# Mish dense layer, 2048 x 512 x 1792: x tiles 2-3 by DMA transpose, eight f tiles first, w1 mostly on the other DMA ring

## Chip, cores, metric

The kernel runs on one core of a Trainium2 chip. The metric is device microseconds (us) of one execution. A profiled execution has a span, which is about 1.4 us shorter than its time. Times within a profile are counted from the start of its span.

## The reference

```python
# x (1, 2048, 512), w1 (512, 1792), b1 (1792), w2 (1792, 512), all bfloat16
def reference(x, w1, b1, w2):
    h = jnp.einsum("bsd,df->bsf", x, w1) + b1
    sp = jnp.log1p(jnp.exp(-jnp.abs(h))) + jnp.where(h > 0, h, jnp.zeros_like(h))
    act = h * jnp.tanh(sp)                 # Mish
    return jnp.einsum("bsf,fd->bsd", act, w2)
```

## The kernel before

The kernel does x in four blocks of 512 rows. For each block it computes `mm1` (w1 against transposed x, 14 f tiles of 4 k steps, 512 columns each), Mish on ScalarE (ACT), then `mm2` (16 matmul chains in all, 14 f steps each). TensorE (PE) needs x transposed. Blocks 1 to 3 come transposed by DMA. Block 0, which everything starts with, is loaded as it is, transposed by TensorE tile by tile (128 rows) and copied out of PSUM by VectorE (DVE) and ACT in turn.

Loads go out on two queues, one issued from SyncE (SP) and one from ACT; I call them the SP ring and the ACT ring. Every load has its own semaphore. A load returns a token, and an engine that needs the data waits on that token:

```python
def wait(self, *tokens):                       # in class Stream
    for tok in tokens:
        ...                                    # cut: None is skipped, known values too
        self.eng.wait_ge(sem, v)

t_xa = load(sp, x_nat[:, 0, :], x0v[0], "s_xa")
t_w1k = [load(act, w1_sb[:, 0:2, 0:F0 * P], w1v[:, 0:2, 0:F0 * P], "s_w1k0")] * 2
t_xb = load(sp, x_nat[:, 1, :], x0v[1], "s_xb")
t_w1k += [load(act, w1_sb[:, 2:4, 0:F0 * P], ..., "s_w1k2")] * 2
t_xc = load(sp, x_nat[:, 2:4, :], x0v[2], "s_xc")
...                                            # cut: b1 on ACT; w1 f 4-7 and f 8-13 on SP
t_w2 = load(sp, w2_sb[:, :, :], w2v, "s_w2")
t_xT = [None]
for s in range(1, NSB):
    t_xT.append(load(sp, xT[:, :, s * SBW:(s + 1) * SBW], x2[s * SBW:(s + 1) * SBW, :], "s_xT%d" % s, True))
```

`t_xT` is a list with one token for each block. In the steady loop `mm1(t)` waits for `t_xT[s]`, the one of its own block. The head of block 0 is written out:

```python
first_mm1([0], by_k(0, 1))                     # four f tiles, x tile 0
part_T([1], t_xb)                              # transpose x tile 1
first_mm1([1], by_k(0, 1))
first_mm1([0, 1], by_k(2))
part_T([2, 3], t_xc)                           # transpose x tiles 2-3
first_mm1([0, 1], by_k(3))
first_mm1([2, 3], by_k(0, 1) + [(f, k) for f in range(F0) for k in (2, 3)])
...                                            # cut: b1 transposed, mish of f 0-3
for t in range(F0, FT):
    mm1(t)                                     # f 4-13, 512 columns each
```

Of the kernel before, what the change touches and what calls it, by code (L numbers as in the profile page):

```python
# [4 lines left out]

P = 128
N_WARM = 16
N_FILL = 3


class Stream:
# [20 lines left out]
def bass_standalone__dense_activation_mish__prompt_kernel(  # L32
# [8 lines left out]
    ACT = mybir.ActivationFunctionType  # L41
    ALU = mybir.AluOpType
    BF, F32 = dt.bfloat16, dt.float32

    _, S, D = x.shape
    F = w1.shape[1]
    KT, FT, SBW = D // P, F // P, 512
    NSB, JT = S // SBW, SBW // P
    assert (S, D, F) == (2048, 512, 1792)
    x2, out2 = x[0], out[0]  # L50
    w1v = w1.rearrange("(k p) f -> p k f", p=P)
    w2v = w2.rearrange("(j p) d -> p j d", p=P)
    F0 = 4

    with ExitStack() as es:
        def sb(name, shape, t):
            return es.enter_context(nc.sbuf_tensor(name, shape, t))

        x_nat = sb("x_nat", [P, JT, D], BF)
        xT = sb("xT", [P, KT, S], BF)  # L60
        w1_sb = sb("w1_sb", [P, KT, F], BF)
        w2_sb = sb("w2_sb", [P, FT, D], BF)
        b1_nat = sb("b1_nat", [FT, P], BF)
        b1_sb = sb("b1_sb", [P, FT], F32)
        ones = sb("ones", [P, P], BF)
        ident = sb("ident", [P, P], BF)
        a_sb = sb("a_sb", [P, NSB * FT, SBW], BF)
        o_sb = sb("o_sb", [P, NSB * JT, D], BF)
        ps = es.enter_context(nc.psum_tensor("ps", [P, 8, 512], F32))

        def sem(name):
            return es.enter_context(nc.semaphore(name))

        sp = Stream(nc.sync, None)
        pe = Stream(nc.tensor, sem("c_pe"))
        dve = Stream(nc.vector, sem("c_dve"))
        act = Stream(nc.scalar, sem("c_act"))
        pool = Stream(nc.gpsimd, sem("c_pool"))

        def load(q, dst, src, name, transpose=False):  # L80
            s = sem(name)
            (q.eng.dma_start_transpose if transpose else q.eng.dma_start)(dst, src).then_inc(s, 16)
            return (s, 16)

        n_pre = len(nc.cur_bb.bb.instructions)



        x0v = [x2[0:P, :], x2[P:2 * P, :], x2[2 * P:SBW, :].rearrange("(p j) d -> p j d", j=2)]
        t_xa = load(sp, x_nat[:, 0, :], x0v[0], "s_xa")  # L90
        t_w1k = [load(act, w1_sb[:, 0:2, 0:F0 * P], w1v[:, 0:2, 0:F0 * P], "s_w1k0")] * 2
        t_xb = load(sp, x_nat[:, 1, :], x0v[1], "s_xb")
        t_w1k += [load(act, w1_sb[:, 2:4, 0:F0 * P], w1v[:, 2:4, 0:F0 * P], "s_w1k2")] * 2
        t_xc = load(sp, x_nat[:, 2:4, :], x0v[2], "s_xc")
        t_b1 = load(act, b1_nat[:, :], b1.rearrange("(j p) -> j p", p=P), "s_b1")
        t_w1 = {}
        for a, b in ((4, 8), (8, FT)):
            t = load(sp, w1_sb[:, :, a * P:b * P], w1v[:, :, a * P:b * P], "s_w1_%d" % a)
            for f in range(a, b):
                t_w1[f] = t  # L100
        t_w2 = load(sp, w2_sb[:, :, :], w2v, "s_w2")
        t_xT = [None]
        for s in range(1, NSB):
            t_xT.append(load(sp, xT[:, :, s * SBW:(s + 1) * SBW], x2[s * SBW:(s + 1) * SBW, :], "s_xT%d" % s, True))

# [5 lines left out]
        act.eng.preload_act_table(ACT.Mish)  # L111


        warm = sb("warm", [P, P], BF)
        pe.wait(dve.mark(nc.vector.memset(warm[:, :], 1.0)))  # L115

        def dummies(n):
            for _ in range(n):
                nc.tensor.matmul(ps[:, 7, 0:P], warm[:, :], warm[:, :], start=True, stop=True)  # L119

        t_cp, t_mm1 = {}, {}
        n_cp = 0

        def part_T(js, tok):

            nonlocal n_cp
            lo, hi = js[0] * P, (js[-1] + 1) * P
            pe.wait(tok)
            for k in range(KT):
                pe.wait(t_cp.get((js[0] - 1, k)))  # L130
                psk = ps[:, k, 0:(hi - lo) // 2].bitcast(BF)
                for n, j in enumerate(js):
                    tr = nc.tensor.transpose(psk[:, n * P:(n + 1) * P], x_nat[:, j, k * P:(k + 1) * P], ident[:, :])  # L133
                t = pe.mark(tr)
                dst = xT[:, k, lo:hi]
                if k % 2 == 0:
                    dve.wait(t)
                    t = dve.mark(nc.vector.tensor_copy(dst, psk))  # L138
                else:
                    act.wait(t)  # L140
                    t = act.mark(act.eng.activation(dst, psk, ACT.Copy))  # L141
                for j in js:
                    t_cp[j, k] = t

        def first_mm1(js, fks):


            cs = slice(js[0] * P, (js[-1] + 1) * P)
            for f, k in fks:
                pe.wait(t_w1k[k], *[t_cp[j, k] for j in js])  # L150
                mm = nc.tensor.matmul(ps[:, 4 + f, cs], w1_sb[:, k, f * P:(f + 1) * P], xT[:, k, cs],  # L151
                                      start=(js[0] == 0 and k == 0), stop=(js[-1] == JT - 1 and k == KT - 1))
                if js[-1] == JT - 1 and k == KT - 1:
                    t_mm1[f] = pe.mark(mm)

        def by_k(*ks):
            return [(f, k) for k in ks for f in range(F0)]

        dummies(N_WARM)
        pe.wait(t_id)  # L160
        part_T([0], t_xa)
        dummies(N_FILL)


        t_mish, t_bank = {}, {}

        def bank1(t):
            return t - F0 if F0 <= t < 2 * F0 else 4 + t % 4

        def mish(t, t_mm):  # L170
            act.wait(t_b1c, t_mm)
            f = t % FT
            t_mish[t] = act.mark(act.eng.activation(a_sb[:, t, :], ps[:, bank1(t), :], ACT.Mish, bias=b1_sb[:, f:f + 1]))  # L173
            t_bank[bank1(t)] = t_mish[t]

        def mm1(t):
            s, f = divmod(t, FT)
            pe.wait(t_bank.get(bank1(t)), t_w1.get(f), t_xT[s])
            for k in range(KT):
                mm = nc.tensor.matmul(ps[:, bank1(t), :], w1_sb[:, k, f * P:(f + 1) * P],  # L180
                                      xT[:, k, s * SBW:(s + 1) * SBW], start=(k == 0), stop=(k == KT - 1))
            mish(t, pe.mark(mm))

        def store(q, i, lo, hi, tok):
            q.wait(tok)
            rows = o0v[:, i % 2, :] if i in (2, 3) else out2[i * P:(i + 1) * P, :]
            q.eng.dma_start(rows[:, lo:hi], o_sb[:, i, lo:hi]).then_inc(s_out, 16)

        s_out = sem("s_out")
        o0v = out2[2 * P:SBW, :].rearrange("(p j) d -> p j d", j=2)  # L190
        n_out = 0

        LC = 384
# [1 line left out]
        def mm2(i):  # L195
            nonlocal n_out
            s, j = divmod(i, JT)
            pe.wait(t_w2)
            last = i == NSB * JT - 1
            parts = [(0, LC, i % 4), (LC, D, (i + 1) % 4)] if last else [(0, D, i % 4)]  # L200
            for lo, hi, bank in parts:
                pe.wait(t_bank.get(bank))
                for f in range(FT):
                    t = s * FT + f
                    pe.wait(t_mish[t])
                    mm = nc.tensor.matmul(ps[:, bank, 0:hi - lo], a_sb[:, t, j * P:(j + 1) * P], w2_sb[:, f, lo:hi],  # L206
                                          start=(f == 0), stop=(f == FT - 1))
                t_mm = pe.mark(mm)
                dve.wait(t_mm)
                t_bank[bank] = dve.mark(nc.vector.tensor_copy(o_sb[:, i, lo:hi], ps[:, bank, 0:hi - lo]))  # L210
                store(sp, i, lo, hi, t_bank[bank])
                n_out += 1


        first_mm1([0], by_k(0, 1))
        part_T([1], t_xb)
        first_mm1([1], by_k(0, 1))
        first_mm1([0, 1], by_k(2))
        part_T([2, 3], t_xc)
        first_mm1([0, 1], by_k(3))  # L220
        first_mm1([2, 3], by_k(0, 1) + [(f, k) for f in range(F0) for k in (2, 3)])
        for k in range(KT):
            t_bank[k] = t_cp[JT - 1, k]
        pe.wait(t_b1, t_bank[3])
        psb1 = ps[:, 3, 0:FT // 2].bitcast(BF)
        dve.wait(pe.mark(nc.tensor.transpose(psb1, b1_nat[:, :], ident[0:FT, 0:FT])))  # L226
        t_bank[3] = t_b1c = dve.mark(nc.vector.tensor_copy(b1_sb[:, :], psb1))  # L227
        for f in range(F0):
            mish(f, t_mm1[f])
        for t in range(F0, FT):  # L230
            mm1(t)
        for s in range(NSB):
            for j in range(JT):
# [41 lines left out]
```

## Time and profile before

| What | Before |
|---|---|
| Time, median of 6 (range) | 105.92 us (105.08 to 106.06) |
| Span of the profiled execution | 103.9 us |
| TensorE busy | 101.1 us, 97% |
| First `mm2` matmul in the chain of waits | 17.41 us |

The page of the kernel before gives busy time by engine, then the span in 40 slices with the busy share in tenths. PEclk is the granted TensorE clock in tenths.

```profile
PE 101.1 (97%) x513; PEld 50.0 (48%) x522; DVE 13.0 (12%) x25; ACT 40.4 (39%) x63; POOL 0.6 (1%) x6
...
PE   8999999999999999999999999999999999999992
...
PEclk9999999999999999999999999999999999999999
```

TensorE is busy everywhere; only the head can give something. The head is read from the timeline (start, duration, engine, line, operation, count) of the kernel before:

```profile
2.28 0.58 PE L133 MATMUL ps<-ident,x_nat 128*128 128x128 bf16 x4
...
3.15 1.03 PE L151 MATMUL ps<-xT,w_sb 128*128 128x128 bf16 x8
...
5.77 0.61 PE L133 MATMUL ps<-ident,x_nat 128*128 128x128 bf16 x8
...
6.22 2.35 PE L151 MATMUL ps<-xT,w_sb 128*128 128x256 bf16 x20
```

Transposes are L133 and the head's own matmuls L151. The next lines are from its chain of waits (start, duration, what):

```profile
8.83 8.58 PE ps L180 x39
17.41 2.16 PE ps L206 x10
```

Line L206 is `mm2`. The first block's `mm1` is worth 56 matmuls of about 0.214 us, which is 12.0 us; TensorE starts on the first x tile at 2.28. That leaves 17.41 - 2.28 - 12.0 = 3.1 us of overhead in the head.

### The profile page before, as it was taken

Reading aid. Unit: us, or ns where it says so; the run is one execution under the profiler, and the core shown is the slowest. Engines: PE = TensorE matmul, PEld = TensorE weight load, DVE = VectorE, ACT = ScalarE, POOL = GpSimd, SP = SyncE. Lnnn points to the kernel's source line nnn. Section 1 sums busy time; section 2 is a strip of 40 time slices with the busy share of each in tenths; the row PEclk is TensorE's granted clock in tenths of the full one; section 3 lists DMA queues with packets and bytes.
Section 4 is the critical chain, followed back from the end, with each engine's and each line's share of the span. In section 5 each row is a group of like instructions: output and inputs, shape, how many; then the busy total and the mean of one; then the engine's idle time right before and its main releaser. Section 6 shows DMA issues by size and latency. Waiting matters only on the chain.

```text
span 103.9 us, 1168 instructions
## 1 busy us (share of the span) xinstructions
PE 101.1 (97%) x513; PEld 50.0 (48%) x522; DVE 13.0 (12%) x25; ACT 40.4 (39%) x63; POOL 0.6 (1%) x6
## 2 busy tenths in 40 slices
PE   8999999999999999999999999999999999999992
PEld 7895444444444444444444444444444444444462
DVE  0310000112220000022220000022112000011223
ACT  2525997000027777200007777500005777700000
POOL 2000000000000000000000000000000000000000
PEclk9999999999999999999999999999999999999999
DMA  5999996951101000010111000001111000001111
GB/s 169 294 349 376 349 187 149 260 146 50 50 7 43 0 6 0 0 50 14 37 50 50 0 3 6 0 0 50 50 50 50 0 0 0 0 6 50 50 50 51
DMA packets 12561, 7.94 MB, mean 76 GB/s; under 512 B 6796, under 2 KB 12428, under 8 KB 12556
## 3 DMA queue, kind: packets, MB, share of 16 engines
q1 hardware_dynamic: 11984, 7.34, 26.5%
q10 hardware_dynamic: 572, 0.53, 1.5%
q8 instruction: 4, 0.07, 0.3%
q14 instruction: 1, 0.01, 0.0%
HBM read 4.20 MB, written 2.10 MB: 61 GB/s over the span
## 4 chain that ended last, share of the span: by engine, by line
PE 97%; issue 1%; DVE 0%
PE ps L206 46%; PE ps L180 43%; PE ps L151 4%; PE ps L119 2%; PE ps L133 1%; DVE o_sb L210 0%; DVE warm L115 0%; PE ps L226 0%
## 5 line engine op out<-in xcount | busy, mean ns | idle before, releaser
L173 ACT ACTIVATE a_sb<-ps,b_sb 128x512 bf16<-128x512 f32 x56 | 37.5, 691 | 46.3 <-PE ps L180 44.2
L206 PE MATMUL ps<-w_sb,a_sb 128*128 128x512 bf16 (+2 forms) x234 | 48.8, 366 | 0.2
L180 PE MATMUL ps<-xT,w_sb 128*128 128x512 bf16 x203 | 45.1, 379 | 0.4 <-issue 0.2
L206 PEld LDWEIGHTS ps<-w_sb,a_sb 128*128 128x128 bf16 x238 | 22.8, 98 | 25.9
L180 PEld LDWEIGHTS ps<-xT,w_sb 128*128 128x128 bf16 x208 | 20.3, 98 | 24.3
L210 DVE CAST o_sb<-ps 128x512 bf16<-128x512 f32 (+2 forms) x17 | 11.2, 660 | 82.3 <-PE ps L206 82.3
L151 PE MATMUL ps<-xT,w_sb 128*128 128x256 bf16 (+1 forms) x40 | 4.7, 282 | 0.0
L151 PEld LDWEIGHTS ps<-xT,w_sb 128*128 128x128 bf16 x40 | 3.7, 113 | 0.7 <-DVE xT L138 0.3
L119 PE MATMUL ps<-warm 128*128 128x128 bf16 x19 | 2.4, 310 | 0.4 <-DVE warm L115 0.4
L141 ACT ACTIVATE xT<-ps 128x128 bf16<-128x128 bf16 (+1 forms) x6 | 1.6, 311 | 2.1 <-PE ps L133 2.1
L119 PEld LDWEIGHTS ps<-warm 128*128 128x128 bf16 x19 | 2.0, 143 | 0.4 <-DVE warm L115 0.4
L138 DVE COPY xT<-ps 128x128 bf16<-128x128 bf16 (+1 forms) x6 | 1.4, 247 | 4.9 <-PE ps L133 4.9
L111 ACT ACT_TABLE_LOAD x1 | 1.3, 1283 | 1.8 <-issue 1.8
L133 PE MATMUL ps<-ident,x_nat 128*128 128x128 bf16 x16 | 1.8, 263 | 0.0
L133 PEld LDWEIGHTS ps<-ident,x_nat 128*128 128x128 bf16 x16 | 1.3, 118 | 0.3 <-issue 0.2
L227 DVE CAST b_sb<-ps 128x14 f32<-128x14 bf16 x1 | 0.2, 173 | 2.1 <-PE ps L226 2.1
L109 POOL TENSOR_SCALAR_AFFINE_SELECT ident<-ones 128x128 bf16<-128x128 bf16 x1 | 0.3, 295 | 0.1
L107 POOL MEMSET ones<- 128x128 bf16 x1 | 0.2, 205 | 0.0
L226 PEld LDWEIGHTS ps<-ident,b_nat 14*128 14x128 bf16 x1 | 0.1, 90 | 0.2 <-issue 0.2
L115 DVE MEMSET warm<- 128x128 bf16 x1 | 0.2, 165 | 0.2 <-issue 0.2
L226 PE MATMUL ps<-ident,b_nat 14*128 14x14 bf16 x1 | 0.2, 177 | 0.0
L260 POOL MEMSET const-bfloat16-1.0<- 128x1 bf16 x1 | 0.1, 103 | 0.0
(3 smaller groups left out, 0.3 us busy)
## 6 DMA issues: line engine op xcount, KB each, us to landing
out_dram<-o_sb SPq DMA_DIRECT2D x15, 128.0 KB, 1.7
w_sb<-in_w_dram SPq DMA_DIRECT2D x1, 1792.0 KB, 12.7
w_sb<-in_w_dram SPq DMA_DIRECT2D x1, 768.0 KB, 8.2
w_sb<-in_w_dram ACTq DMA_DIRECT2D x2, 256.0 KB, 3.6
w_sb<-in_w_dram SPq DMA_DIRECT2D x1, 512.0 KB, 6.5
x_nat<-in_x_dram SPq DMA_DIRECT2D x2, 128.0 KB, 2.6
x_nat<-in_x_dram SPq DMA_DIRECT2D x1, 256.0 KB, 3.9
out_dram<-o_sb SPq DMA_DIRECT2D x1, 96.0 KB, 1.6
```

What stands on the lines that cost most here:

```text
L109: t_id = pool.mark(pool.eng.affine_select(ident[:, :], ones[:, :], pattern=[[1, P]], compare_op=ALU.is_equal, fill=0.0, base=0, channel_mu ...
L111: act.eng.preload_act_table(ACT.Mish)
L119: nc.tensor.matmul(ps[:, 7, 0:P], warm[:, :], warm[:, :], start=True, stop=True)
L133: tr = nc.tensor.transpose(psk[:, n * P:(n + 1) * P], x_nat[:, j, k * P:(k + 1) * P], ident[:, :])
L138: t = dve.mark(nc.vector.tensor_copy(dst, psk))
L141: t = act.mark(act.eng.activation(dst, psk, ACT.Copy))
L151: mm = nc.tensor.matmul(ps[:, 4 + f, cs], w1_sb[:, k, f * P:(f + 1) * P], xT[:, k, cs], start=(js[0] == 0 and k == 0), stop=(js[-1] == JT ...
L173: t_mish[t] = act.mark(act.eng.activation(a_sb[:, t, :], ps[:, bank1(t), :], ACT.Mish, bias=b1_sb[:, f:f + 1]))
L180: mm = nc.tensor.matmul(ps[:, bank1(t), :], w1_sb[:, k, f * P:(f + 1) * P], xT[:, k, s * SBW:(s + 1) * SBW], start=(k == 0), stop=(k == KT ...
L206: mm = nc.tensor.matmul(ps[:, bank, 0:hi - lo], a_sb[:, t, j * P:(j + 1) * P], w2_sb[:, f, lo:hi], start=(f == 0), stop=(f == FT - 1))
L210: t_bank[bank] = dve.mark(nc.vector.tensor_copy(o_sb[:, i, lo:hi], ps[:, bank, 0:hi - lo]))
L226: dve.wait(pe.mark(nc.tensor.transpose(psb1, b1_nat[:, :], ident[0:FT, 0:FT])))
```

## The change

The intent is to spend less TensorE time on transposes and waits in the head. TensorE transposes only x tiles 0 and 1. Tiles 2-3 come by a small DMA transpose (256 rows). Meanwhile tiles 0-1 are taken against eight f tiles instead of four, k by k, in all eight PSUM banks. The middle part of w1 (f 4-7) moves to the ACT ring, so that the small transpose has less ahead of it on the SP ring. SP holds that transpose back until w1's k 2-3 part has landed. The core of the diff:

```diff
-        t_w1k = [load(act, w1_sb[:, 0:2, 0:F0 * P], w1v[:, 0:2, 0:F0 * P], "s_w1k0")] * 2
+        t_w1k = [load(act, w1_sb[:, k, 0:F0 * P], w1v[:, k, 0:F0 * P], "s_w1k%d" % k) for k in range(2)]
...
+        for k in (0, 2):
+            t_w1m += [load(act, w1_sb[:, k:k + 2, F0 * P:2 * F0 * P], w1v[:, k:k + 2, F0 * P:2 * F0 * P], "s_w1m%d" % k)] * 2
+        sp.wait(t_w1k[2])
+        t_xT = [load(sp, xT[:, :, 2 * P:SBW], x2[2 * P:SBW, :], "s_xT0", True)]
...     # w1 f 8-13, w2 and the transposes of blocks 1-3 follow on the SP ring, appended to t_xT as before
-                pe.wait(t_w1k[k], *[t_cp[j, k] for j in js])
+                pe.wait((t_w1k if f < F0 else t_w1m)[k])
+                if js[0] == 0 and k == 0:
+                    pe.wait(t_bank.get(bank1(f)))
+                pe.wait(*([t_cp[j, k] for j in js] if js[0] < 2 else t_xT))
...
-        first_mm1([0], by_k(0, 1))
-        part_T([1], t_xb)
-        ...
+        first_mm1([0], by_k(0, 0))
+        part_T(1, t_xb)
+        first_mm1([0], by_k(0, 1))
+        first_mm1([1], by_k(0, 0, 1))
+        first_mm1([0, 1], by_k(0, 2))
+        ...     # b1
+        first_mm1([0, 1], by_k(0, 3))
+        ...
+        first_mm1([0, 1], by_k(F0, *range(KT)))
+        first_mm1([2, 3], [(f, k) for f in range(2 * F0) for k in range(KT)])
+        for t in range(2 * F0, FT):
             mm1(t)
```

Cut: `N_FILL` 3 to 2, the copies all on DVE, b1 loaded on the SP ring, plain rows for the output.

## The prediction

> **What bounds the kernel now.** TensorE: busy 101.1 of 103.9 us on the page, 97% of the chain of waits. In steady state 512-column matmuls start about 0.214 us apart with hardly a gap (busy by windows: 59.7 of 60 us), so only the head can give. In the chain mm2 starts at 17.41 us. The first block's mm1 is 56 such matmuls, 12.0 us; x arrives at 2.28. Overhead: 17.41 - 2.28 - 12.0 = 3.1 us. The timeline divides it: transposes 0.58 + 0.43 + 0.45, fillers 0.32, the 16 128-column matmuls about 1.0 over their ideal share (with a wait of 0.26 for a copy), the bias transpose and waits about it 0.27.
>
> The early matmuls are slow by clock: 128-column starts lie 107 ns apart up to about 5.3 us, then 256-column ones take 109 ns. That agrees with the Trainium skill, "TensorE: Matmul & The Clock Gate", Part 1 (half rate until the array has been busy for some microseconds); the page's granted-clock row doesn't show it.
>
> **Removed.** Eight transposes (0.45 us), one filler (0.11), the ACT copies (which waited for the table load and cost PE the 0.26), most of the wait about the bias (0.2). **Added.** 256-column matmuls in place of 512 for eight f tiles: 2 x 109 against 214 ns, about 0.1 us in all. DVE makes all eight copies at 225 ns, behind PE's work.
>
> **Moved.** x tiles 2-3 come by a 256 KB DMA transpose, issued once w1's k 2-3 part has landed (estimate: 4.0 us). The before trace holds three 512 KB transposes: queue time 2.2 and 3.0 us for the two not held up, landing 4.4 and 5.5 us after the start of issue. The first sat in the queue 11.9 us, until the w2 load ahead of it on that ring had drained. Now little is ahead of it on its ring, which is why w1 goes to the other. At half the size I estimate 3 to 4 us from issue: landing at 7.0 to 8.2 us.
>
> PE's timeline from those spacings: first transposes 2.28, first mm1 2.95, tile 1's transposes 3.4, 128-column work till 5.1, 256-column work on tiles 0-1 (24 matmuls) till 7.9. The transposed data is needed at about 7.9 us, nearly when I expect it: a stall of 0 to 0.6 us, 0.2 in the middle. Then 32 x 109 ns and 24 x 214 ns: mm2 starts at 16.6 without a stall, 16.8 with; before 17.4. ACT (691 ns per Mish) falls behind in the k-major stage but frees its banks just in time (f 12's at about 14.7, wanted 14.9). w1's rest (about 10 us, wanted 11.4) and w2 (about 15, wanted 16.6) should be in time.
>
> **Predicted.** The gain is all on the critical path, but only 0.8 us less the stall: 105.1 us, range 104.3 to 106.2. Faster by over 2%: 0.02; within 2%: 0.94; slower by over 2%: 0.04.
>
> **Right or wrong by the profile.** First mm2 at 16.5 to 17.0 in the chain; a wait for the xT DMA of under 0.6 us ahead of the tiles 2-3 matmuls; the small transpose landing 3 to 4 us after issue; no ACT copies; steady state unchanged.
>
> **What would make it wrong.** The transpose held up by the other ring's w1 traffic too, or landing later than 8.5 us: each us late is a us lost, and past 8.8 us the gain is gone. w2 pushed behind 16.6 us. Or the clock rising earlier or later than 5.3 us.

## The result

| What | Before | After |
|---|---|---|
| Time, median of 6 (range) | 105.92 us (105.08 to 106.06) | 122.94 us (122.14 to 124.72) |
| Ratio | | 1.159 (95% interval 1.152 to 1.166) |
| Span of the profiled execution | 103.9 us | 123.1 us (a slow run, 124.48 us) |
| First `mm2` matmul in the chain of waits | 17.41 us | 36.61 us |

A ratio is the mean time of one kernel's fast runs over that of the other's in the same rounds, so it is not quite the ratio of the medians. The outputs of all kernels here are correct.

The page of the changed kernel. Its profiled run is one of the two slow ones (of the six runs, the two more than 1.5% above the fastest); none of its fast runs was traced:

```profile
PE 103.7 (84%) x520; PEld 52.7 (43%) x529; DVE 12.9 (10%) x28; ACT 39.5 (32%) x57; POOL 0.6 (1%) x6
...
PE   8890000089999999999999999999999999999994
...
PEclk9999655555999999999999999999999999999999
```

There is one hole of five slices, and from its second slice on, for six slices, the granted clock is about half. Everything after that is as before. The waits of the changed kernel (who waited for whom: us in total, times, longest):

```profile
PE ps L145 <- DMA xT<-in_x_dram: 16.2, 1, 16.2
```

Its timeline on TensorE:

```profile
2.46 0.59 PE L133 MATMUL ps<-ident,x_nat 128*128 128x128 bf16 x4 [0.18 <-DMA x_nat<-in_x_dram]
...
5.78 1.00 PE L145 MATMUL ps<-xT,w_sb 128*128 128x256 bf16 x4 [0.36 <-DMA w_sb<-in_w_dram]
...
6.67 2.35 PE L145 MATMUL ps<-xT,w_sb 128*128 128x256 bf16 x20
25.21 6.22 PE L145 MATMUL ps<-xT,w_sb 128*128 128x256 bf16 x32 [16.20 <-DMA xT<-in_x_dram]
31.48 5.13 PE L174 MATMUL ps<-xT,w_sb 128*128 128x512 bf16 x23
36.45 3.83 PE L198 MATMUL ps<-w_sb,a_sb 128*128 128x512 bf16 x17
```

The loss is a single wait, ahead of the matmuls on tiles 2-3, and the slow stage after it: 32 matmuls from 25.21 to 31.48, so 196 ns each, where 256 columns take 109 ns at full clock. 16.2 us of stall and 32 x (0.196 - 0.109) = 2.8 us of slow clock make 19.0 of the 19.2 us by which the two spans differ. These are the sizes in a slow run; e2 and e3 below were traced in fast runs and show the same wait and the same slow stage.

Which transfer did it wait for? The page says only "xT". The chain of waits of the changed kernel shows the queue of transposes behind it:

```profile
5.75 1.32 SPq L82
...
8.28 9.94 SPq L82
18.22 0.04 issue
18.27 2.53 SPq L82
20.80 0.04 issue
20.84 4.24 DMA xT<-in_x_dram
25.08 0.14 issue
25.21 6.22 PE ps L145 x32
```

The entry at 5.75 is the small transpose of tiles 2-3; by the trace's landing records it was complete at 9.09, when TensorE had just got there. The wait ended with the entry at 20.84: the transpose of block 3, the last of four. That points to one expression in the diff: `pe.wait(*(... else t_xT))` unpacks the whole list, and when these matmuls are put down the list holds four tokens. So tiles 2-3 of block 0 wait for blocks 1, 2 and 3 as well. The waits of the built program say the same: that matmul waits on `s_xT0`, `s_xT1`, `s_xT2` and `s_xT3`.

### The profile page after: what moved, and what is told of

Its sections match the earlier page's. It is cut to its first block, busy times and chain, and to the rows that moved or that the text cites. A ratio compares the mean times of both kernels' runs of the same rounds, so it can differ in the third digit from the quotient of the medians.

```text
span 123.1 us, 1184 instructions
## 1 busy us (share of the span) xinstructions
PE 103.7 (84%) x520; PEld 52.7 (43%) x529; DVE 12.9 (10%) x28; ACT 39.5 (32%) x57; POOL 0.6 (1%) x6
## 4 chain that ended last, share of the span: by engine, by line
PE 78%; SPq 12%; DMA 7%; issue 1%; ACTq 1%; DVE 0%
PE ps L198 39%; PE ps L174 33%; SPq L82 12%; PE ps L145 5%; DMA w_sb<-in_w_dram 4%; DMA xT<-in_x_dram 3%; ACTq L82 1%; DVE o_sb L202 0%
## 5 line engine op out<-in xcount | busy, mean ns | idle before, releaser
L167 ACT ACTIVATE a_sb<-ps,b_sb 128x512 bf16<-128x512 f32 x56 | 38.2, 687 | 67.8 <-PE ps L174 44.5
L198 PE MATMUL ps<-w_sb,a_sb 128*128 128x512 bf16 (+2 forms) x233 | 48.8, 366 | 0.3
L174 PE MATMUL ps<-xT,w_sb 128*128 128x512 bf16 x188 | 41.7, 379 | 0.2
L198 PEld LDWEIGHTS ps<-w_sb,a_sb 128*128 128x128 bf16 x238 | 22.8, 98 | 25.9
L174 PEld LDWEIGHTS ps<-xT,w_sb 128*128 128x128 bf16 x192 | 18.8, 98 | 22.4
L145 PE MATMUL ps<-xT,w_sb 128*128 128x256 bf16 (+1 forms) x72 | 11.5, 338 | 16.6 <-DMA xT<-in_x_dram 16.2
L145 PEld LDWEIGHTS ps<-xT,w_sb 128*128 128x128 bf16 x72 | 8.4, 128 | 19.2 <-issue 16.4
L134 DVE COPY xT<-ps 128x128 bf16<-128x128 bf16 x8 | 1.2, 217 | 2.8 <-PE ps L133 2.8
L133 PE MATMUL ps<-ident,x_nat 128*128 128x128 bf16 x8 | 1.2, 307 | 0.2 <-DMA x_nat<-in_x_dram 0.2
L133 PEld LDWEIGHTS ps<-ident,x_nat 128*128 128x128 bf16 x8 | 0.8, 137 | 0.4 <-issue 0.4
```

What stands on the lines that cost most here:

```text
L133: dve.wait(pe.mark(nc.tensor.transpose(psk, x_nat[:, j, k * P:(k + 1) * P], ident[:, :])))
L134: t_cp[j, k] = dve.mark(nc.vector.tensor_copy(xT[:, k, j * P:(j + 1) * P], psk))
L145: mm = nc.tensor.matmul(ps[:, bank1(f), cs], w1_sb[:, k, f * P:(f + 1) * P], xT[:, k, cs], start=(js[0] == 0 and k == 0), stop=(js[-1] == ...
L167: t_mish[t] = act.mark(act.eng.activation(a_sb[:, t, :], ps[:, bank1(t), :], ACT.Mish, bias=b1_sb[:, f:f + 1]))
L174: mm = nc.tensor.matmul(ps[:, bank1(t), :], w1_sb[:, k, f * P:(f + 1) * P], xT[:, k, s * SBW:(s + 1) * SBW], start=(k == 0), stop=(k == KT ...
L198: mm = nc.tensor.matmul(ps[:, bank, 0:hi - lo], a_sb[:, t, j * P:(j + 1) * P], w2_sb[:, f, lo:hi], start=(f == 0), stop=(f == FT - 1))
```

## The experiments

The first theory, the "list theory": the loss is the wait for all four transposes, plus the slow clock that the idle time brings. Its rival, the "transpose theory": the small DMA transpose, or the new order of the rings, is itself what is late. The first four kernels tell these apart. The own-wait kernel (e1) came out 0.8% slower than before, not faster, so a second group asks where the predicted 0.8 us went.

| Kernel | Median (us) | Ratio to before, 95% interval |
|---|---|---|
| after | 122.94 | 1.159 (1.152 to 1.166) |
| e1_own_only | 106.47 | 1.008 (1.004 to 1.013) |
| e2_own_and_next | 118.35 | 1.122 (1.115 to 1.128) |
| e3_before_waits_all | 122.33 | 1.157 (1.150 to 1.164) |
| e4_keep_busy | 121.47 | 1.151 (1.145 to 1.157) |
| g1_no_hold | 109.11 | 1.024 (1.017 to 1.031) |
| g2_short_hold | 105.10 | 0.995 (0.990 to 0.999) |
| g3_w2_other_ring | 112.37 | 1.061 (1.055 to 1.068) |
| h1_w2_halves | 105.09 | 0.995 (0.993 to 0.998) |
| h2_w1m_own_ring | 106.60 | 1.006 (1.001 to 1.011) |

The medians are of all runs.

### e1_own_only: wait for the small transpose alone

```diff
-                pe.wait(*([t_cp[j, k] for j in js] if js[0] < 2 else t_xT))
+                pe.wait(*([t_cp[j, k] for j in js] if js[0] < 2 else t_xT[:1]))
```

> The changed kernel, but TensorE waits ahead of the tiles 2-3 matmuls for their own transposed load alone, not for all four transposes. List theory (the stall comes of waiting for the last of four transposes, which lands at 25.1 us in the changed kernel's trace): the wait shrinks from 16.2 us to under 0.5 us (the small transpose landed at 9.05, TensorE was ready at 8.9), the clock stays up, and the time falls to 105.5 to 107.5 us; it need not reach the predicted 105.1, since in that trace w1's last part lands at 13.3 us and would be wanted at 12.6. Transpose theory (the small DMA transpose is itself what came late, or the ring order starves it): the wait stays above 5 us and the time above 112 us.

106.47 us. One token in place of four takes back 16.5 of the 17.0 us. The small transpose lands at 8.47 in this trace, the long wait is gone and the granted clock is 1.0. What is left is a new wait, at the start of `mm2`, on the timeline of this kernel:

```profile
6.03 6.16 PE L145 MATMUL ps<-xT,w_sb 128*128 128x256 bf16 x52
12.21 5.34 PE L174 MATMUL ps<-xT,w_sb 128*128 128x512 bf16 x24
18.74 5.57 PE L198 MATMUL ps<-w_sb,a_sb 128*128 128x512 bf16 x25 [1.20 <-DMA w_sb<-in_w_dram]
```

TensorE waits 1.2 us for w2. The list theory stands; that the change would then win does not.

### e2_own_and_next: wait for two of the four

```diff
-                pe.wait(*([t_cp[j, k] for j in js] if js[0] < 2 else t_xT))
+                pe.wait(*([t_cp[j, k] for j in js] if js[0] < 2 else t_xT[:2]))
```

> The changed kernel, with TensorE waiting for the first two of the four transposes. List theory: the stall ends when the second one lands, at about 20.9 us in the changed kernel's trace (8.28 + 12.6), 4.2 us before the fourth, and the clock is still halved by the long idle time: 118 to 119.5 us. Transpose theory: no change from the 122.9 us.

118.35 us, as the list theory said. The wait in this kernel's timeline:

```profile
19.34 6.37 PE L145 MATMUL ps<-xT,w_sb 128*128 128x256 bf16 x32 [11.18 <-DMA xT<-in_x_dram]
```

It ends at 19.34; the second transpose landed at 19.21 in this trace (I had expected 20.9, from the changed kernel's). The stall follows the last token waited for.

### e3_before_waits_all: the kernel before with the long wait added

```diff
+        pe.wait(*t_xT)
         first_mm1([2, 3], by_k(0, 1) + [(f, k) for f in range(F0) for k in (2, 3)])
```

> The kernel before, untouched but for one wait: TensorE waits for its three transposes (blocks 1 to 3) ahead of the matmuls on tiles 2-3. List theory: the last lands at 22.4 us in the trace of before, TensorE gets there at about 6.9, so 15.5 us of stall and about 3 us of halved clock after it: 122.5 to 125.5 us. If the DMA transpose of tiles 2-3, the k-major order or the moved w1 loads made the loss, this kernel, which has none of them, loses little more than what a late wait costs: under 112 us.

122.33 us, a little under the 122.5 expected. The kernel before, with none of the change in it, becomes as slow as the changed one by this one wait. Its timeline:

```profile
22.29 3.57 PE L151 MATMUL ps<-xT,w_sb 128*128 128x256 bf16 x16 [15.70 <-DMA xT<-in_x_dram]
```

So the wait is enough to make the loss, and by e1 the loss is gone without it. The transpose theory is out as an explanation of the 17 us.

### e4_keep_busy: the long wait, but TensorE not idle

```diff
+        zero = sb("zero", [P, 2 * P], BF)
+        t_zero = dve.mark(nc.vector.memset(zero[:, :], 0.0))
...
+        pe.wait(t_zero)
+        for _ in range(140):
+            nc.tensor.matmul(ps[:, 7, 0:2 * P], warm[:, :], zero[:, :], start=False, stop=False)
         first_mm1([2, 3], [(f, k) for f in range(2 * F0) for k in range(KT)])
```

`zero` is a tile of zeros, so these matmuls add nothing to the bank.

> The changed kernel with its long wait, and 140 matmuls of 256 columns that add zeros, put ahead of the wait so that TensorE is busy until about 24.2 us. If the halved clock after the stall (granted clock 0.50, 32 matmuls in 6.22 us) comes of the idle time, the clock stays up, those 32 take 3.5 us and the time falls by about 2.7 us, to 119.5 to 121 us. If it comes of something else in this stage, the time stays at 122 to 124.7.

121.47 us, half a microsecond above the range expected. The mechanism showed: the clock stayed at 1.0 in all four runs, and the stage after the wait ran at full rate in this kernel's timeline.

```profile
8.21 15.45 PE L225 MATMUL ps<-zero,warm 128*128 128x256 bf16 x140
24.52 3.65 PE L147 MATMUL ps<-xT,w_sb 128*128 128x256 bf16 x32 [0.86 <-DMA xT<-in_x_dram]
...
33.19 7.07 PE L200 MATMUL ps<-w_sb,a_sb 128*128 128x512 bf16 x32
```

From trace to trace `mm2` starts 3.3 us earlier here (33.19 against 36.45). Of that, 0.7 us is the last transpose, which landed at 24.38 instead of 25.08; the other 2.6 us is the clock. In times the saving is smaller: 3.0 us against the profiled slow run, but 1.1 us against the mean of the four fast runs of the changed kernel (122.6 us).

A likely reason for the miss is that I took the 2.8 us from the profile of a slow run. The changed kernel's six runs differ in how long the clock stayed down. The share of the clock that each run lists gives the time at half rate as 2 x (1 - share) x span: 13.5 us for 122.38 us (share 0.944), 17.1 us for 123.49 (0.930) and 20.5 us for 124.72 (0.917). These are close to 4, 5 and 6 times 3.41 us. The clock records in the traces give the same steps: one stretch at half rate of 17.07 us in the changed kernel's, of 13.65 in e2's, of 3.41 in g1's. The Trainium skill, "TensorE: Matmul & The Clock Gate", Part 1 (What's actually happening), states a free-running window of 3413 ns in which TensorE's activity sets its clock, and these numbers agree with that length. How much of the half-rate time fell on work in the fast runs is not on record. The clock is the small part of the loss, 1 to 3 us and different from run to run, and the idle time is the large one.

### g1_no_hold: where did the predicted gain go?

In e1's trace SP stands still until 5.04 us, when w1's k 2-3 part has landed; the small transpose, w1's last part and w2 are all issued after that, and w2 lands at 18.7. This kernel, like all that follow, keeps e1's correction and takes the hold away.

```diff
-        sp.wait(t_w1k[2])
```

> The own-wait kernel (106.47 us, 0.8% slower than before; mm2 started at 18.74 us there after a 1.2 us wait for w2, which landed at 18.7) without the hold that keeps the small transpose, w1's last part and w2 back until w1's k 2-3 has landed (5.0 us). Hold theory: w2 is late because everything behind the hold starts 3.5 us later; without it w2 lands at 15 to 16.5 us, the wait for it is gone, mm2 starts at 17.0 to 17.6 and the time is 105.0 to 105.7, level with before or slightly better. Ring theory (w2 is late because a DMA transpose stands ahead of it on its ring and delays what follows): w2 gains much less than 3 us. Rival cost: the early transpose takes the DMA engines from w1's first parts, and TensorE waits in the head; then 106 or more.

109.11 us, worse. (Three of the six runs are slow; the ratio in the table uses the other three, 107.8 to 108.77 us, and is 1.024 where e1's is 1.008. The profile is of a slow run, 109.44 us, so the sizes that follow are those of a slow run.) The rival cost that I had named is what came: the early transpose and the w1 parts on the ACT ring are in flight together, and both are late. w1's parts for k 2-3 of f 0-3, then for f 4-7, land at 5.7, 7.8 and 10.1 us (in e1 at 5.0, 5.7 and 6.4), and the transpose that was issued at 1.41 lands at 10.3. TensorE waits three times on the timeline of this kernel:

```profile
5.79 0.61 PE L144 MATMUL ps<-xT,w_sb 128*128 128x256 bf16 x4 [0.99 <-DMA w_sb<-in_w_dram]
...
7.80 1.05 PE L144 MATMUL ps<-xT,w_sb 128*128 128x256 bf16 x8 [0.91 <-DMA w_sb<-in_w_dram]
10.18 6.21 PE L144 MATMUL ps<-xT,w_sb 128*128 128x256 bf16 x40 [1.33 <-DMA w_sb<-in_w_dram]
```

w2 landed at 18.4, so it gained almost nothing by an issue about 3.6 us earlier. By the packet records the SP ring moved only the transpose's packets, and few at a time, from 3.5 us until 8. With this order of the rings a hold helps; the question is how long.

### g2_short_hold: hold only until w1's first k has landed

```diff
-        sp.wait(t_w1k[2])
+        sp.wait(t_w1k[0])
```

> The own-wait kernel with the hold shortened to the landing of w1's first k (2.9 us in its trace, instead of 5.0). Hold theory: w2 lands some 2 us earlier, at 16.5 to 17, before TensorE wants it at about 17.5: 105.0 to 105.7 us. Ring theory: w2 lands within 1 us of before and 106 us or more remains.

105.10 us, 0.5% faster than before, with an interval that just excludes 1. The small transpose is issued at 2.77, as w1's first k lands (the 2.9 that I gave for e1 was misread: it is 2.50 there), and itself lands at 8.55. w2 lands at 17.40; I had expected 16.5 to 17, but it is in time, as this kernel's chain of waits shows no DMA between 2.46 us and `mm2` (L198):

```profile
12.57 5.12 PE ps L174 x23
17.69 5.61 PE ps L198 x26
```

So the predicted time is reached once two things are mended: the wait for the list, and a hold that is too long by some 2 us. The start of `mm2` is not: 17.69 here, where 16.5 to 17.0 was predicted and 17.41 is that of before.

### g3_w2_other_ring: w2 on the ACT ring

```diff
-        t_w2 = load(sp, w2_sb[:, :, :], w2v, "s_w2")
+        t_w2 = load(act, w2_sb[:, :, :], w2v, "s_w2")
```

> The own-wait kernel with w2 loaded on the other ring, behind w1's middle parts, so that it is behind neither the hold nor the transpose. Both theories expect w2 by 13 to 15 us, no wait for it, mm2 at 17.0 to 17.6 us and 105.0 to 105.7 us, unless w1's last part, which now shares the engines with w2, comes later than TensorE wants it (about 12.2 us); then a wait appears there instead.

112.37 us: my expectation was wrong. w2 is indeed early, at 13.1 us, but now the small transpose is late, on this kernel's timeline of SP's queue and of TensorE:

```profile
6.20 1.32 SPq L82 DMA_TRANSPOSE xT<-in_x_dram  x1
```

```profile
13.71 5.33 PE L145 MATMUL ps<-xT,w_sb 128*128 128x256 bf16 x32 [4.63 <-DMA xT<-in_x_dram]
```

It lands at 13.66, 7.5 us after its issue, where in e1 and in the changed kernel it took 3.4 and 3.3. In the records of the DMA packets its first packets of 256 B run only after 10.5 us, 4.3 us after the issue and when w2's packets on the other ring thin out; until then the ACT ring moves about 170 to 190 packets of 1 KB each half microsecond, and the SP ring none. In e1 and in the changed kernel the first packets run 1.4 us after the issue. So w2 in flight on the other ring held the transpose up. The two kernels differ in w2 alone, but in its time as well as in its ring: past the hold, it is issued at 2.55 us and not at 7.03. Which of the two matters was not tested.

### h1_w2_halves: the short hold, with w2 in two loads

```diff
-        t_w2 = load(sp, w2_sb[:, :, :], w2v, "s_w2")
+        t_w2 = [load(sp, w2_sb[:, j:j + 7, :], w2v[:, j:j + 7, :], "s_w2_%d" % j) for j in (0, 7)]
...
-            pe.wait(t_w2)
...
-                    pe.wait(t_mish[t])
+                    pe.wait(t_mish[t], t_w2[f // 7])
```

> The short-hold kernel (105.1 us, w2 landed at 17.4 us in its trace, only just before TensorE wanted it) with w2 loaded in two halves, each with its own semaphore, so that mm2 starts on the first half. If w2's landing costs the short-hold kernel something in those executions in which the clock rises early, the median falls by 0.1 to 0.5 us, to 104.6 to 105.0. If TensorE alone sets the time there, it stays at 105.1 within 0.2.

105.09 us, the same as g2. The first half of w2 is there at 14.1 us, so w2 no longer matters, and nothing is gained. In its profile the last wait for a DMA in the head is one of 0.2 us for w1's k 2-3 at 5.6 us; after that TensorE's own work sets the time until `mm2`, which starts at 17.1 on its timeline and at 17.24 in its chain of waits:

```profile
12.06 5.18 PE ps L174 x24
17.24 12.09 PE ps L197 x56
```

### h2_w1m_own_ring: w1's middle part on the SP ring

```diff
-        sp.wait(t_w1k[2])
...
-            t_w1m += [load(act, w1_sb[:, k:k + 2, ...
+            t_w1m += [load(sp, w1_sb[:, k:k + 2, ...
```

> The own-wait kernel with w1's middle parts on the transposes' own ring, ahead of the small transpose, and no hold. If a transpose waits in the queue until what is ahead of it on its own ring has drained (as the first transpose of before seems to behind w2), its queue time is no longer 1.3 us but lasts to about the landing of w1's middle parts (5 to 6 us), it lands at 8 to 9.5 us, w2 at 17 to 19, and the time is 105 to 106.5 us: the other ring was not needed to avoid a loss. If it doesn't wait, its queue entry ends near 4 us and it lands by 7.

106.60 us, with runs from 105.27 to 106.84. The SP queue on this kernel's timeline:

```profile
1.42 0.91 SPq L82 DMA_DIRECT2D w_sb<-in_w_dram  x2
2.38 1.30 SPq L82 DMA_TRANSPOSE xT<-in_x_dram  x1
```

The transpose's queue entry takes 1.30 us with 512 KB of w1 ahead of it on its ring, no longer than in e1 (1.32) with nothing ahead. So my reading of the kernel before, that its first transpose stood in the queue for 11.9 us until w2 ahead of it had drained, does not hold as a general rule. It does fit the large transposes: in all eleven traces the queue entry of the first of them ends 0.2 to 0.4 us before the plain load ahead of it lands (w2; in g3 w1's last part). Why the small one is let through, by its own size or by the 512 KB ahead of it in place of 3 MB, stays open. It lands at 8.45, as early as in e1 and later than the 7 expected for this case, and w2 at 17.27. What costs here is that w1's k 2-3 part is pushed to 6.6 us, and TensorE waits 1.3 us for it. By the means of fast runs h2 is 1.2 us slower than g2 (106.30 and 105.13), so that much at most is what the other ring is worth here; g1 and g2, which differ in the hold alone, are 3.0 us apart (108.15 and 105.13).

## Why the prediction was wrong

- **What bounds the kernel: right.** All differences lie in the head; from `mm2` on the traces are alike.
- **The step that failed** is in "PE's timeline from those spacings: ... The transposed data is needed at about 7.9 us, nearly when I expect it: a stall of 0 to 0.6 us". I priced the wait as one for the small transpose. The diff waits for a list, and the list holds four tokens at that point. The stall was 16.2 us. e1 (own token: 106.47), e2 (two tokens: 118.35) and e3 (the same wait put into the kernel before: 122.33) show it from three sides. No duration was needed to see it: the list of waits of the built program has four semaphores at that matmul.
- **"each us late is a us lost"** was too low for a long stall. After it TensorE ran at half rate until the clock came back; e4 puts this at 2.6 us between two traces, and at 1.1 us in time against fast runs.
- **The small transpose "landing 3 to 4 us after issue": right** where the ACT ring was nearly drained, 3.3 us in the changed kernel and 3.4 in e1; with more in flight beside it, it took 5.3 to 8.9 us (h1, g2, h2, g3, g1). **Its issue at 4.0 us was mis-sized:** it was 5.75, 5.04 in e1, since w1's k 2-3 part landed that late. **"w2 (about 15...)" was mis-sized** too: 18.5 in the changed kernel, 18.7 in e1. That term cost 1.2 us of TensorE's time there and ate the predicted gain of 0.6 to 0.8 us.
- **"Now little is ahead of it on its ring, which is why w1 goes to the other": the reading did not hold for the small transpose.** h2 shows that 512 KB ahead on the own ring do not lengthen the queue entry, and g3 that what is in flight on the other ring does delay the transpose.
- **"The clock rising earlier or later than 5.3 us" was a fair warning.** The first matmul at full rate came between 3.7 and 6.9 us in the eleven traces. In g2's trace it came at 6.9 and `mm2` still started at 17.5; in h1's at 5.9 and `mm2` started at 17.1, against 17.25 in the timeline of before with the clock up at 5.2.
- **The predicted time came out in the end, but not shown by the predicted way.** With both faults mended, the same design gives 105.1 us, which is 0.5% under before. Yet `mm2` starts at 17.69 (g2) and 17.24 (h1) in the chains of the mended kernels, not at 16.5 to 17.0. In both traces the clock also rose later than in that of before, and nothing on record separates that from the design, so part of the agreement may be luck. I had put the whole gain into the range, and no chance to speak of on a fault in the code that the change added.

## What to carry to other kernels

Before pricing a wait, list every semaphore that it names in the built program: a helper that is handed a list waits for the last member of it, and the cost of the wait is that of the latest transfer, not of the one that the author had in mind. When a page names a tensor as the releaser ("xT") and several transfers fill it, find which of them landed as the wait ended. In these runs the landing of a load depended on what else was in flight, on both rings (3.3 to 8.9 us for the small transpose), so after such a fault is mended measure where loads should be held back; here the length of the hold decided between 107.9 us (none, fast runs), 105.1 (short) and 106.5 (long).

## What the Trainium skill lacked or had wrong

- "DMA: Bandwidth & Descriptors", Rules for kernel authors: "A transpose next to ordinary DMAs needs nothing." All outputs were correct, which agrees as to safety, and the sentence is about safety. What it lacks is the time: with w2 in flight on the other ring (g3) the first packets of the transpose ran 4.3 us after its issue and it landed after 7.5 us, against 3.4 us; with w1's parts for k 2-3 and f 4-7 in flight beside it from the start (g1, a slow run) it landed after 8.9 us and w1 itself 3.7 us later than in e1.
- The same page, "Issuing engines are not separate DMA queues", states that DMAs issued from different engines interleave on the same 16 DMA engines. In g3 they did not for 4.3 us: from 6.20 to 10.5 us the ACT ring moved about 170 to 190 packets each half microsecond, and the SP ring, with the transpose issued on it, none (in e1 1.4 us pass from issue to first packet). Whether the SP ring had work ready in that time is not recorded. In g1 the packets of the two rings did mix.
- "TensorE: Matmul & The Clock Gate", Part 1, puts the rise to full clock at about 4 us of sustained matmuls, with a spread of 0.5 us from run to run. The spread here was wider: in the eleven traces the first matmul at full rate came 3.3 to 6.5 us after the first matmul (which ran at 0.39 us); in e1, whose timeline shows TensorE without a listed wait up to then, it was 6.0 us. The page's window of 3413 ns agrees with half-rate times of 13.5, 17.1 and 20.5 us.
- No page that I read says that the granted clock listed with a profile can show 1.0 while the array still runs at half rate at the start: in the kernel before it reads full from the first slice, and 128-column matmuls started 107 ns apart until 5.2 us and 56 ns apart after. The trace itself has no clock record until 5.21 us (e1, g2 and h2 have none at all), and the listing counts what is not recorded as full. The nearest is that page's caveat that the trace's clock events can be unreliable.
